# A kernel of a scan and two MoE layers: the range test of the first MoE's weights is moved into the second MoE

## The chip, the cores and the metric

The kernel runs on one core of one Trainium2 chip. A core has five engines that this text names: PE (TensorE, matrix products), DVE (VectorE), ACT (ScalarE), POOL (GpSimd) and SP (SyncE, which issues nearly all transfers). The metric is the device time of one execution in microseconds (us).

## The reference

Inputs are float32 arrays for the scan; the MoE weights arrive as float64, and the kernel converts them itself.

```python
def _attn_ref(r, k, v, w, a, b):          # 4 batches, 8 heads, 768 steps, head size 40
    for t in range(S):
        y[:, :, t] = np.einsum('bhd,bhde->bhe', rt, state)
        Sa = np.einsum('bhde,bhe->bhd', state, at)
        state_decay = state * wt[:, :, None, :] - np.einsum('bhd,bhe->bhde', Sa, bt)
        state = state_decay + np.einsum('bhd,bhe->bhde', vt, kt)

def _moe_ref(x, w1, w2, w3, w_out):       # 3072 tokens, 320 -> 768 -> 320
    h = np.maximum(np.maximum(x @ w1, x @ w2), x @ w3)
    return h @ w_out

def _moe2_ref(x, w_in, w_out):            # 3072 tokens, 320 -> 2048 -> 320
    h = x @ w_in
    sp = np.where(h > 20.0, h, np.log1p(np.exp(np.minimum(h, 20.0))))
    g = h * np.tanh(sp)
    return g @ w_out
```

The output is the scan, then the first MoE, then the second.

## The kernel before

The scan is cut into 48 chunks of 32 steps (24 for each half of the batch). `Attention.pre` (L230 on) prepares pairs of chunks; `Attention.solve` inverts a triangular system of four pairs on DVE (L303 to L314); `Attention.chain` runs one chunk through PE, ACT and DVE. The first solve and the first four `pre` run before the first chunk. In `pre`, PE writes a product `m` into PSUM (L275), ACT copies half of it to `ab` (L280) and DVE transposes the other half to `akT` (L282); `solve` begins with DVE's transpose of `ab` (L303).

The first MoE's weights are 24 tiles: 18 of 128 x 3 x 128 for w1, w2, w3 and 6 of 128 x 320 for w_out. `from64` (L575 on) loads a tile of float64 words into `raw` (SP, L579), tests its range, and turns it into float32 with ACT (L593), DVE (L594, L595) and POOL (L597). The parts `put` then splits it into a high and a low part for the float32 products (ACT L606, POOL L612, DVE L651; for w_out L718 and L721). The test is a pair of ACTIVATEs with an accumulated sum: Square of the high words (L587) and Exp of the result (L588). The sums go to columns of the tile `g_t`, and `Gate.count` compares them with their bounds at the very end: if any bound is broken, a slow general version runs instead. So the test's result is needed only at the end of the kernel.

`pipelined(moe1.weights(), 2)` starts a new tile every second step, and `fill` takes three steps of it in each of the five slots of a chunk, so the conversion lies beside chunks 0 to 3. From chunk 4 on the first MoE runs beside the scan (`Moe1.group`). The second MoE's weights are converted by the same `from64` beside the last chunks and the first MoE's tail, their tests writing into the staging tile (`ct`, `t`).

The second MoE is six groups of 512 tokens (`Moe2.group`). A group has 16 blocks `m`: eight matmuls of 512 columns into `cps` (four PSUM banks, L661 to L665), an elementwise chain that alternates between ACT (L969, L972, L973, L974, L983) and DVE (L970, L976, L977, L979, L984), and twelve matmuls of 320 columns into `cops` (L988 to L990). `cps` of a block is free after DVE's L979. The next group's x is loaded by SP (L933) and split by POOL (L941, L942); the output is copied by DVE (L1024) and ACT (L1026) and stored by SP (L1028).

PE and DVE keep the written order up to the end of the scan. ACT does too, but for chunks 0 to 3, where a conversion's step may be put ahead of a step that is written earlier. Elsewhere a scheduler orders the instructions when the kernel is built, by its own estimate of times. Every engine then runs its list in order, and so does SP's queue.

Of the kernel before, what the change touches and what calls it, by code (L numbers as in the profile page):

```python
# [8 lines left out]
F32 = mybir.dt.float32  # L9
F32R = mybir.dt.float32r  # L10
I32 = mybir.dt.int32
AF = mybir.ActivationFunctionType
ALU = mybir.AluOpType
PSUM = bass.MemoryType.PSUM

B, H, S, D = 4, 8, 768, 40
DM, F1, F2 = H * D, 768, 2048
# [136 lines left out]
class Attention:  # L154
# [74 lines left out]
    def load(self, n):  # L229
        self.load_a(n)  # L230
        self.load_k(n)
# [333 lines left out]
def finish(it):  # L565
    for _ in it:
        pass
# [5 lines left out]
    return stage  # L573


def from64(nc, stage, src, n, cols, gate, put, beside=False, junk=None):

    raw, t = stage(n, cols)
    nc.sync.dma_start(out=raw, in_=src.bitcast(I32).rearrange("p k (f w) -> p k f w", w=2))  # L579
    for _ in range(3 if junk else 2):  # L580
        yield
    low, high = raw[:, :, :, 0], raw[:, :, :, 1]
    tf = t.bitcast(F32)
    q = junk.tile([128, n, cols], F32, name="junk", tag="junk") if junk else tf


    nc.scalar.activation(out=q, in_=high.bitcast(F32), func=AF.Square, accum_out=gate.le(2.0 ** 33))  # L587
    nc.scalar.activation(out=q, in_=q, func=AF.Exp, scale=-(2.0 ** 20), accum_out=gate.le(0.25))  # L588
    yield
    if beside:  # L590
        nc.vector.tensor_scalar(out=low, in0=low.bitcast(mybir.dt.uint32), scalar1=2.0 ** -29, scalar2=None, op0=ALU.mult)
    else:
        nc.scalar.activation(out=low, in_=low.bitcast(mybir.dt.uint32), func=AF.Copy, scale=2.0 ** -29)  # L593
    nc.vector.tensor_scalar(out=t, in0=high, scalar1=3, scalar2=0x3FFFFFF8, op0=ALU.logical_shift_left, op1=ALU.bitwise_and)  # L594
    nc.vector.scalar_tensor_tensor(out=t, in0=high, scalar=-0x40000000, in1=t, op0=ALU.bitwise_and, op1=ALU.bitwise_or)  # L595
    yield
    nc.gpsimd.tensor_tensor(out=t, in0=t, in1=low, op=ALU.add)  # L597
    yield
    yield from put(tf)
# [31 lines left out]
class Weights:  # L631
# [9 lines left out]
        return (x[:, 0:256].rearrange("p (k f) -> p k f", k=2), x[:, 256:512].rearrange("p (k f) -> p k f", k=2),  # L641
                x[:, 512:640])

    def load(self, j, stage, beside=False, pool=False, junk=None):
        nc = self.nc
        h, l, m = self.parts(j)

        def put(t):
            copy(nc, m, t[:, 2], pool)
            yield from split_to(nc, h, l, t[:, 0:2], pool)  # L650
            nc.vector.tensor_tensor(out=m[64:128], in0=t[64:128, 2], in1=m[64:128].bitcast(F32), op=ALU.subtract)  # L651

        return from64(nc, stage, self.src[j], 3, 128, self.gate, put, beside, junk)

    def mm(self, ps, j, x):

# [20 lines left out]
class Moe1:  # L677
    N = 2 * GT

    def __init__(self, ctx, tc, A, xs, x1, gate):  # L680
        self.tc, self.nc, self.A, self.xs, self.x1, self.gate = tc, tc.nc, A, xs, x1, gate

        def pool(name, bufs, ctx=ctx, **kw):
            return ctx.enter_context(tc.tile_pool(name=name, bufs=bufs, side="left", reuse_waits="tile", **kw))

        self.pool = pool
        wp = pool("b_w", 1)
        self.stage = ExitStack()
        self.tmp = staged(pool("b_t", 4, ctx=self.stage))
        self.junk = pool("b_j", 1, ctx=self.stage, space=PSUM)  # L690
        ws = [wp.tile([128, 6, 640], F32R, name="b" + n) for n in ("w1", "w2", "w3")]
        self.w = [Weights(self.nc, A[n], [w[:, j] for j in range(6)], gate) for n, w in zip(("w1", "w2", "w3"), ws)]

        self.o = wp.tile([128, 6, 2, DM], F32R, name="bo").rearrange("p k s f -> p k (s f)")
# [14 lines left out]
    def weights(self):  # L709
        for j in range(6):  # L710
            for w in self.w:
                yield w.load(j, self.tmp, junk=self.junk)
        for j in range(6):
            yield from64(self.nc, self.tmp, self.A["wo"][j], 1, DM, self.gate, lambda t, j=j: self.put_out(t[:, 0], j), junk=self.junk)

    def put_out(self, t, j):
        nc, o = self.nc, self.o[:, j]
# [102 lines left out]
class Moe2:  # L820
# [168 lines left out]
            nc.tensor.matmul(out=self.acc[j], lhsT=gh[:, cs], rhs=self.ol[m], start=False, stop=False)  # L989
            nc.tensor.matmul(out=self.acc[j], lhsT=gl[:, cs], rhs=self.oh[m], start=False, stop=(m == 15))  # L990

    def group(self, q):

        tc, nc = self.tc, self.nc
        acc = self.acc = [self.psb.tile([128, DM], F32, name=f"cops{j}") for j in range(4)]
        rest = iter(()) if q else self.conversions()
        under, self.begun = self.begun, []
        early = len(under)
        for m in range(16 + 3):
            if early <= m < 16 and (q, m) not in self.ps:  # L1000
                self.product(q, m)
            for i, g in enumerate(under):
                if i >= early or m >= i + 1:
                    next(g, None)
            if early <= m < 16:
                under.append(self.activation(q, m))
                next(under[-1])
            if m == 8 and q < 5:
                self.load_x(q + 1)
            if m == 11 and q < 5:  # L1010
                self.split_x(q + 1)

            with tc.issue_after(self.newest):
                next(rest, None)
                if m == 11:
                    finish(rest)
        del self.x[q]
        o = self.p2.tile([128, 4, DM], F32, name="o")
# [158 lines left out]
def program(tc, A, out, only=None):  # L1177
    nc = tc.nc
# [6 lines left out]
    with ExitStack() as c_mid:  # L1185
        keep = c_mid.enter_context(tc.tile_pool(name="keep", bufs=1, side="right"))
        moe2 = Moe2(tc, A, x1, out, gate)
        with ExitStack() as c_moe1:
# [55 lines left out]
                        moe2.begin(i - 18, moe1.spare(i % 2))  # L1244
            finish(rest)
        moe2.open_work(c_mid)
        for q in range(6):
            moe2.group(q)
    if only:
        only(att, xs, x1)  # L1250
    n, total = gate.count()
# [21 lines left out]
```

## Time and profile before

| What | Value |
|---|---|
| median of 3 runs | 1072.19 us |
| lowest and highest | 1071.51 and 1073.66 us |
| span of the profiled execution, first to last instruction | 1070.9 us |
| what lies between the span and the median | 1.3 us |
| PE busy | 912.0 us (85% of the span) |
| DVE busy | 878.3 us (82%) |
| ACT busy | 731.2 us (68%) |
| POOL busy | 339.6 us (32%) |
| moved by DMA | 87.03 MB, 81 GB/s in the mean |

Of the profiled execution the page gives the span; its own time is that span and what lies around it, for which the last difference is taken. The shares are means over stages with different limits, so the stretches below say more than this table. A wait is named after what ended it.

### The profile page before, as it was taken

The page shows a single profiled execution, that of the slowest core. Times are in us where ns is not written, and L with a number is a line of the kernel's source. Part 1 is how long each engine was busy: PE and PEld are TensorE (multiplying, and loading weights), DVE is VectorE, ACT ScalarE, POOL GpSimd, SP SyncE. Part 2 cuts the span into 40 slices and gives each one's busy share as a digit, 9 for nine tenths or more (in the row PEclk, how much of TensorE's full clock was granted, in tenths as well). Part 3 has the DMA queues.
Part 4 walks back from the last instruction along what each step waited for, and adds up shares of the span by engine and source line. Part 5 has one row for each costly group of instructions (what it writes and reads, how often), then busy time and mean ns, then how long its engine had stood idle before and what let it go on. Part 6 is the DMA issues. An engine that isn't in the chain of part 4 may idle for free.

```text
span 1070.9 us, 34069 instructions
## 1 busy us (share of the span) xinstructions
PE 912.0 (85%) x14098; PEld 816.2 (76%) x14098; DVE 878.3 (82%) x1698; ACT 731.2 (68%) x1886; POOL 339.6 (32%) x422
## 2 busy tenths in 40 slices
PE   1313456899999999999999999979999999999996
PEld 1212345888888888888998888878889998888995
DVE  7589979978968987886688666899988989898875
ACT  4638864465566665656667777677787887878874
POOL 7437894333233242323114334681201002010000
PEclk9999999999999999999999999999999999999999
DMA  8415532243433434333334443530100000010000
GB/s 211 134 62 159 144 91 64 71 128 84 114 101 100 110 96 113 94 88 97 81 85 104 132 134 90 173 108 5 30 25 31 25 30 26 1 54 1 25 1 28
DMA packets 110615, 87.03 MB, mean 81 GB/s; under 512 B 72740, under 2 KB 89764, under 8 KB 110452
## 3 DMA queue, kind: packets, MB, share of 16 engines
q1 hardware_dynamic: 109712, 84.54, 29.0%
q8 instruction: 113, 1.85, 0.8%
q14 instruction: 50, 0.41, 0.1%
q10 hardware_dynamic: 740, 0.23, 0.1%
HBM read 72.16 MB, written 12.58 MB: 79 GB/s over the span
## 4 chain that ended last, share of the span: by engine, by line
PE 56%; DVE 23%; ACT 9%; issue 4%; DMA 4%; POOL 2%; SPq 0%; ACTq 0%; DVEq 0%; POOLq 0%
PE cops L988 5%; PE cops L989 5%; PE cops L990 5%; PE ys L436 4%; PE bps L661 4%; PE cps L661 4%; PE cps L662 4%; PE cps L663 4%; PE bps L812 3%; DVE T L310 3%; PE bps L662 3%; PE bps L663 3%; DVE tv L308 3%; PE cgps L353 2%; PE cps L665 2%
## 5 line engine op out<-in xcount | busy, mean ns | idle before, releaser
L661 PE MATMUL bps<-bxh,bw 128*128 128x256 f32 x432 | 139.9, 325 | 2.3 <-DVE mx L771 1.4
L662 PE MATMUL bps<-bxl,bw 128*128 128x256 f32 x432 | 124.1, 287 | 3.2 <-DVE bxl L674 3.2
L663 PE MATMUL bps<-bxh,bw 128*128 128x256 f32 x432 | 122.8, 284 | 0.0
L774 POOL TENSOR_TENSOR hl<-mx,hh 128x256 fp32r<-128x256 f32 x72 | 56.7, 787 | 172.8 <-ACT hh L773 145.2
L310 DVE TENSOR_TENSOR T<-T,tv 128x31 f32<-128x31 f32 (+15 forms) x186 | 86.4, 464 | 6.4
L661 PEld LDWEIGHTS bps<-bxh,bw 128*128 128x128 f32 x432 | 82.5, 191 | 11.4 <-DVE mx L771 2.0
L252 POOL TENSOR_TENSOR ax<-ax,pp 40x256 f32<-40x256 f32 x96 | 75.4, 805 | 45.1 <-DMA ax<-in_A_dram 16.1
L662 PEld LDWEIGHTS bps<-bxl,bw 128*128 128x128 f32 x432 | 83.2, 193 | 5.4 <-DVE bxl L674 5.4
L288 POOL TENSOR_SCALAR_AFFINE_SELECT ax<-akT 32x256 f32<-32x256 f32 x96 | 51.3, 535 | 104.6 <-DVE akT L282 100.6
L663 PEld LDWEIGHTS bps<-bxh,bw 128*128 128x128 f32 x432 | 83.1, 192 | 0.0
L972 ACT ACTIVATE e<-e 128x512 f32<-128x512 f32 x93 | 58.6, 630 | 33.3 <-DVE e L970 33.0
L436 PE MATMUL ys<-rs,ls 128*40 128x72 f32 x1536 | 64.8, 241 | 14.6 <-DVE rs L423 9.9
L812 PE MATMUL bps<-hh,bo 128*128 128x256 f32 x360 | 74.9, 291 | 1.5 <-ACT mx L769 1.5
L984 DVE TENSOR_TENSOR gl<-e,gh 128x512 fp32r<-128x512 f32 x93 | 65.8, 708 | 12.5 <-ACT gh L983 12.5
L976 DVE SCALAR_TENSOR_TENSOR e<-e,r 128x512 f32<-128x512 f32 x93 | 66.0, 710 | 11.7 <-ACT r L974 11.4
L275 PE MATMUL m<-bk,ax 40*32 40x64 f32 x1536 | 43.1, 254 | 38.1 <-DMA bk<-in_KB_dram 14.6
L436 PEld LDWEIGHTS ys<-rs,ls 128*40 128x40 f32 x1536 | 55.6, 126 | 22.0 <-DVE rs L423 9.4
L441 DVE TENSOR_TENSOR sv<-ys,pp 40x320 f32<-40x320 f32 x92 | 44.7, 486 | 32.1 <-PE ys L436 31.4
L941 POOL CAST cxh<-cxl 128x1536 fp32r<-128x1536 f32 x5 | 9.1, 1814 | 193.8 <-DMA cxl<-x 193.8
L771 DVE TENSOR_TENSOR mx<-bps,mx 128x256 f32<-128x256 f32 x144 | 60.3, 419 | 11.6 <-ACT mx L769 7.7
L977 DVE SCALAR_TENSOR_TENSOR e<-e,r 128x512 f32<-128x512 f32 x93 | 68.2, 734 | 1.0
L308 DVE TENSOR_TENSOR tv<-tr,T 128x31 f32<-128x31 f32 (+15 forms) x186 | 67.1, 361 | 1.9
(214 smaller groups left out, 3108.3 us busy)
## 6 DMA issues: line engine op xcount, KB each, us to landing
bk<-in_KB_dram SPq DMA_DIRECT2D x24, 448.0 KB
sv<-in_SV_dram SPq DMA_DIRECT2D x96, 80.0 KB
raw<-in_w_dram SPq DMA_DIRECT2D x18, 384.0 KB
w<-in_W_dram SPq DMA_DIRECT2D x21, 231.0 KB
v<-in_VT_dram SPq DMA_DIRECT2D x48, 96.0 KB
rs<-in_RT_dram SPq DMA_DIRECT2D x48, 96.0 KB
cxl<-x SPq DMA_DIRECT2D x12, 384.0 KB
raw<-in_wo_dram SPq DMA_DIRECT2D x13, 320.0 KB
```

What stands on the lines that cost most here:

```text
L252: nc.gpsimd.tensor_tensor(out=xv[:, h], in0=xv[:, h], in1=P[ro, h, 0:C], op=ALU.mult)
L308: nc.vector.tensor_tensor(out=tv, in0=abT[:, s, s + 1:C].unsqueeze(2).to_broadcast([128, n, s + 1]), in1=T[:, s, 0:s + 1].unsqueeze(1).to_ ...
L310: nc.vector.tensor_tensor(out=T[:, s + 1:C, 0:s + 1], in0=T[:, s + 1:C, 0:s + 1], in1=tv, op=ALU.subtract)
L436: nc.tensor.matmul(out=self.ys[64 * y:64 * y + 40, p, 0:72], lhsT=l[:, y, p], rhs=r_[:, :, 4 * (p % 4) + 2 * (1 - y) + p // 4], start=True ...
L661: nc.tensor.matmul(out=ps, lhsT=h[:, k], rhs=xh[:, k], start=(k == 0), stop=False)
L662: nc.tensor.matmul(out=ps, lhsT=h[:, k], rhs=xl[:, k], start=False, stop=False)
L663: nc.tensor.matmul(out=ps, lhsT=l[:, k], rhs=xh[:, k], start=False, stop=False)
L771: after(1, lambda ps=ps, mx=mx: nc.vector.tensor_tensor(out=mx, in0=ps, in1=mx, op=ALU.max))
L812: nc.tensor.matmul(out=pss[d][rows], lhsT=lhsT, rhs=rhs, start=first, stop=last)
L976: nc.vector.scalar_tensor_tensor(out=e, in0=e, scalar=1.0, in1=r, op0=ALU.add, op1=ALU.mult)
L977: nc.vector.scalar_tensor_tensor(out=e, in0=e, scalar=-float(np.sqrt(8.0)), in1=r, op0=ALU.add, op1=ALU.mult)
L984: nc.vector.tensor_tensor(out=gl, in0=e, in1=gh.bitcast(F32), op=ALU.subtract)
```

## The change

The test becomes a function of its own, `test64`. With `later=True`, `from64` leaves it out, and with it one of its steps; the first MoE's 24 tiles are converted in that way. A new generator, `Moe1.tests`, loads each of the 24 tiles once more into the second MoE's staging tiles and does the same two ACTIVATEs there, with the result in `t`. `Moe2.group` takes a step of it in each of its 19 turns in groups 1 to 5, a new tile every third step. The PSUM tile `junk` goes.

```diff
+def test64(nc, high, q, gate):
+
+    nc.scalar.activation(out=q, in_=high.bitcast(F32), func=AF.Square, accum_out=gate.le(2.0 ** 33))
+    nc.scalar.activation(out=q, in_=q, func=AF.Exp, scale=-(2.0 ** 20), accum_out=gate.le(0.25))
+
+
+def tested(nc, stage, src, n, cols, gate):
 
     raw, t = stage(n, cols)
     nc.sync.dma_start(out=raw, in_=src.bitcast(I32).rearrange("p k (f w) -> p k f w", w=2))
-    for _ in range(3 if junk else 2):
+    for _ in range(3):
+        yield
+    test64(nc, raw[:, :, :, 1], t.bitcast(F32), gate)
+
+
+def from64(nc, stage, src, n, cols, gate, put, beside=False, later=False):
...
+    for _ in range(3 if later else 2):
         yield
     low, high = raw[:, :, :, 0], raw[:, :, :, 1]
     tf = t.bitcast(F32)
-    q = junk.tile([128, n, cols], F32, name="junk", tag="junk") if junk else tf
-
-
-    nc.scalar.activation(out=q, in_=high.bitcast(F32), func=AF.Square, accum_out=gate.le(2.0 ** 33))
-    nc.scalar.activation(out=q, in_=q, func=AF.Exp, scale=-(2.0 ** 20), accum_out=gate.le(0.25))
-    yield
+    if not later:
+        test64(nc, high, tf, gate)
+        yield
...
-        self.junk = pool("b_j", 1, ctx=self.stage, space=PSUM)
...
+    def tests(self, stage):
+
+        for j in range(6):
+            for n in ("w1", "w2", "w3"):
+                yield tested(self.nc, stage, self.A[n][j], 3, 128, self.gate)
+        for j in range(6):
+            yield tested(self.nc, stage, self.A["wo"][j], 1, DM, self.gate)
...
-    def group(self, q):
+    def group(self, q, rest):
...
-        rest = iter(()) if q else self.conversions()
...
                 next(rest, None)
-                if m == 11:
+                if m == 11 and q == 0:
                     finish(rest)
...
+        tests = pipelined(moe1.tests(moe2.stage), 3)
         for q in range(6):
-            moe2.group(q)
+            moe2.group(q, tests if q else moe2.conversions())
+        finish(tests)
```

At three places this is how the lists of instructions change. The lines of the changed kernel are numbered anew: L587 and L588 are L578 and L579 there, L593 is L605, L933 is L952, L969 is L988.

ACT before the first solve, before the change (`m_330` and `m_374` are the products of the third and the fourth `pre`):

```order
L587 ACTIVATE junk,g_t<-raw 128x384
L260 ACTIVATE tr_167,g_t<-tr_167 104x16x32
L593 ACTIVATE raw<-raw 128x384
L246 ACTIVATE Q,g_t<-Q 104x512
L588 ACTIVATE junk,g_t<-junk 128x384
L593 ACTIVATE raw<-raw 128x384
L280 COPY ab_155<-m_330 128x256
```

and the same place with the change, down to the copy of the fourth:

```order
L605 ACTIVATE raw<-raw 128x384
L260 ACTIVATE tr_164,g_t<-tr_164 104x16x32
L246 ACTIVATE Q,g_t<-Q 104x512
L605 ACTIVATE raw<-raw 128x384
L280 COPY ab_152<-m_327 128x256
L605 ACTIVATE raw<-raw 128x384 x2
L280 COPY ab_152<-m_371 128x256
```

The tests ahead of the first copy are gone; between the two copies stood, before, six more instructions of tests besides the two L593, and now only these two.

ACT in the second MoE, behind the first group's output copy, before the change:

```order
L969 ACTIVATE e<-cps 128x512
L972 ACTIVATE e<-e 128x512
L983 CAST gh<-e 128x512
L973 ACTIVATE r<-e 128x512
L969 ACTIVATE e<-cps 128x512
L974 ACTIVATE r<-r,half 128x512
```

and with the first of the 24 tests:

```order
L992 ACTIVATE r<-e 128x512
L988 ACTIVATE e<-cps 128x512
L578 ACTIVATE t_12898,g_t<-raw 128x384
L993 ACTIVATE r<-r,half 128x512
L579 ACTIVATE t_12898,g_t<-t_12898 128x384
L1002 CAST gh<-e 128x512
```

A test's two ACTIVATEs stand between the steps of the elementwise chain, in most places one pair for every three blocks, and now and then two within one block; the last pair stands in the list a little before the fifth group's output copy.

SP's queue from the first group's stores to the second's, before the change:

```order
L1028 DMA out_dram<-o 128x2x320 x2
L933 DMA cxl<-x_0_76 128x3x256
L933 DMA cxl<-x_1_77 128x3x256
L1028 DMA out_dram<-o 128x2x320 x2
L933 DMA cxl<-x_2_78 128x3x256
```

and with the change:

```order
L1046 DMA out_dram<-o 128x2x320 x2
L585 DMA raw<-in_w_dram 128x768 x4
L952 DMA cxl<-x_0_76 128x3x256
L952 DMA cxl<-x_1_77 128x3x256
L585 DMA raw<-in_w_dram 128x768 x3
L1046 DMA out_dram<-o 128x2x320 x2
```

Seven loads of weights stand among a group's loads of x and its stores, and each needs one of three staging buffers, which the test of three tiles earlier frees.

## Rows read from the trace of the kernel before

**Rows 1.** Busy time by stretch: length, busy us (instructions) by engine, granted clock, DMA share, GB/s.
```profile
69.00:170.00 101.00, 43.36 (x1146) 34.93 (x1138) 87.16 (x136) 75.11 (x242) 80.17 (x92) 1.00 0.45 126
170.00:200.00 30.00, 22.80 (x405) 20.07 (x408) 26.93 (x57) 12.13 (x38) 9.72 (x14) 0.89 0.28 70
...
300.00:400.00 100.00, 96.64 (x2222) 87.66 (x2220) 82.03 (x185) 62.63 (x195) 36.63 (x58) 1.00 0.40 101
...
790.00:848.00 58.00, 58.00 (x323) 52.31 (x322) 51.31 (x83) 47.78 (x83) 5.84 (x2) 1.00 0.08 26
```

**Rows 2.** Lines L587 and L588, tests: duration ns min/median/max, first and last start.
```profile
L587 ACT ACTIVATE junk<-raw x24: 438/508/535, 32.0 to 146.8; 128x384 f32<-128x384 f32 x18, 128x320 f32<-128x320 f32 x6
L587 ACT ACTIVATION_READ_ACCUMULATOR junk<-raw x24: 185/188/207, 32.5 to 147.2; 128x1 f32 x24
...
L588 ACT ACTIVATE junk<-junk x24: 415/474/488, 34.2 to 147.7; 128x384 f32<-128x384 f32 x18, 128x320 f32<-128x320 f32 x6
```

**Rows 3.** ACT's groups by shape, whole run: busy us, mean ns | idle before.
```profile
L587 ACT ACTIVATE t<-raw 128x384 f32<-128x384 f32 x6 | 3.3, 553 | 3.1 <-DMA raw<-in_wi_dram 3.1
...
L588 ACT ACTIVATE t<-t 128x384 f32<-128x384 f32 x6 | 3.1, 515 | 0.0
```

**Rows 4.** Instructions in time order, 31 to 41 us: start us, length us [idle before <-releaser].
```profile
31.99 0.54 ACT L587 ACTIVATE junk<-raw 128x384 f32<-128x384 f32 x1
...
34.20 0.47 ACT L588 ACTIVATE junk<-junk 128x384 f32<-128x384 f32 x1
...
35.12 0.35 ACT L280 COPY ab<-m 128x256 f32<-128x256 f32 x1
...
36.08 2.49 PE L275 MATMUL m<-bk,ax 40*32 40x64 f32 x64 [2.99 <-DVE akT L282]
...
39.85 0.36 ACT L280 COPY ab<-m 128x256 f32<-128x256 f32 x1
...
40.30 0.45 DVE L282 STREAM_TRANSPOSE akT<-m 128x256 f32<-128x256 f32 x1 [3.70 <-ACT ab L280]
```

**Rows 5.** Groups by line, 69 to 170 us.
```profile
L587 ACT ACTIVATE junk<-raw 128x384 f32<-128x384 f32 (+1 forms) x20 | 9.9, 497 | 2.8 <-DMA raw<-in_w_dram 2.6
```

**Rows 6.** DVE's waits, 69 to 160 us: us in total, times, longest.
```profile
DVE bw L651 <- ACT bw L606: 4.0, 3, 1.8
DVE sv L441 <- PE ys L436: 2.6, 2, 1.9
...
DVE w L256 <- ACT Q L246: 0.5, 1, 0.5
```

**Rows 7.** ACT in time order, second MoE's first groups.
```profile
778.58 0.73 ACT L1026 COPY o<-cops 128x320 f32<-128x320 f32 x2
...
784.19 0.63 ACT L972 ACTIVATE e<-e 128x512 f32<-128x512 f32 x1
...
787.06 0.63 ACT L972 ACTIVATE e<-e 128x512 f32<-128x512 f32 x1
...
836.23 0.74 ACT L1026 COPY o<-cops 128x320 f32<-128x320 f32 x2
```

**Rows 8.** Time order around two of POOL's splits of x: ACT; POOL, DVE and PE.
```profile
831.50 0.63 ACT L972 ACTIVATE e<-e 128x512 f32<-128x512 f32 x1 [2.43 <-DVE e L970]
...
943.18 3.84 POOL L942 TENSOR_TENSOR cxl<-cxl,cxh 128x1536 fp32r<-128x1536 f32 x1
...
943.67 3.89 DVE L977 SCALAR_TENSOR_TENSOR e<-e,r 128x512 f32<-128x512 f32 x1
947.60 0.69 DVE L979 SCALAR_TENSOR_TENSOR e<-e,cps 128x512 f32<-128x512 f32 x1
...
948.34 0.50 PE L661 MATMUL cps<-cxh,c_ax 128*128 128x512 f32 x1 [0.70 <-DVE e L979]
```

**Rows 9.** SP's issue of the last x, and PE's first matmul on it.
```profile
936.86 1.19 SPq L933 DMA_DIRECT2D cxl<-x  x2
...
995.97 0.40 PE L661 MATMUL cps<-cxh,c_ax 128*128 128x512 f32 x1
```

More of the change, by code (lines that the diff above doesn't have):

```diff
@@ L573, in staged @@
     return stage
-def from64(nc, stage, src, n, cols, gate, put, beside=False, junk=None):
+def test64(nc, high, q, gate):
+    nc.scalar.activation(out=q, in_=high.bitcast(F32), func=AF.Square, accum_out=gate.le(2.0 ** 33))
+    nc.scalar.activation(out=q, in_=q, func=AF.Exp, scale=-(2.0 ** 20), accum_out=gate.le(0.25))
+def tested(nc, stage, src, n, cols, gate):
     raw, t = stage(n, cols)
     nc.sync.dma_start(out=raw, in_=src.bitcast(I32).rearrange("p k (f w) -> p k f w", w=2))
-    for _ in range(3 if junk else 2):
+    for _ in range(3):
+        yield
+    test64(nc, raw[:, :, :, 1], t.bitcast(F32), gate)
+def from64(nc, stage, src, n, cols, gate, put, beside=False, later=False):
+    raw, t = stage(n, cols)
+    nc.sync.dma_start(out=raw, in_=src.bitcast(I32).rearrange("p k (f w) -> p k f w", w=2))
+    for _ in range(3 if later else 2):
         yield
@@ L642, in parts, with load @@
                 x[:, 512:640])
-    def load(self, j, stage, beside=False, pool=False, junk=None):
+    def load(self, j, stage, beside=False, pool=False, later=False):
         nc = self.nc
@@ L651, in put @@
             nc.vector.tensor_tensor(out=m[64:128], in0=t[64:128, 2], in1=m[64:128].bitcast(F32), op=ALU.subtract)
-        return from64(nc, stage, self.src[j], 3, 128, self.gate, put, beside, junk)
+        return from64(nc, stage, self.src[j], 3, 128, self.gate, put, beside, later)
     def mm(self, ps, j, x):
@@ L711, in weights @@
             for w in self.w:
-                yield w.load(j, self.tmp, junk=self.junk)
+                yield w.load(j, self.tmp, later=True)
         for j in range(6):
-            yield from64(self.nc, self.tmp, self.A["wo"][j], 1, DM, self.gate, lambda t, j=j: self.put_out(t[:, 0], j), junk=self.junk)
+            yield from64(self.nc, self.tmp, self.A["wo"][j], 1, DM, self.gate, lambda t, j=j: self.put_out(t[:, 0], j), later=True)
+    def tests(self, stage):
[4 more added lines that the diff above has]
+            yield tested(self.nc, stage, self.A["wo"][j], 1, DM, self.gate)
     def put_out(self, t, j):
```

## The prediction

> **What bounds the kernel now.** I read the busy time by stretch first [rows 1]. The reader is to see two regimes. From 69 to 170 us, while the first MoE's weights are converted beside the first attention chunks, no engine is full: DVE is busy for 87.16 of 101 us, POOL for 80.17, ACT for 75.11 and PE for 43.36. From 300 us on PE is the limit (96.64 of 100), and in the second MoE it is not idle in a whole group (58.00 of 58), with DVE at 51.31 and ACT at 47.78. The change takes ACT work out of the first regime and puts it into the second.
>
> Then the cost of a test. Before, the two ACTIVATEs last 508 and 474 ns in the median, and an accumulator read of 188 ns follows [rows 2]; with the same read behind the second that is 1.36 us, and 24 tiles make 32.6 us of ACT. In the second MoE the result goes to the staging tile t and no longer to the PSUM tile junk; the tests that already write t last 553 and 515 ns for 128x384 [rows 3], so a tile costs 1.44 us there, and 24 make at most 34.7 us.
>
> **The change part by part.**
>
> *1. The start.* The first triangular solve cannot begin before the fourth pre-step is done. Its chain runs through ACT [rows 4]. Before the copy ab at 35.12 stand an L587 of 0.54 and an L588 of 0.47; without them the copy, and the matmuls m behind it at 36.08, come 1.0 us sooner. These matmuls end at 36.08 + 2.49 = 38.57, but the next copy ab starts only at 39.85, for ACT is still at tests: 1.3 us more. DVE's transpose akT at 40.30, which waited 3.70 us, hangs on that copy, and the solve follows it. So the solve starts 1.0 + 1.3 - 0.1 (a hand-over) = 2.2 us sooner. It is pure DVE work until the first chunk, so I carry the whole 2.2 us. Lower end 1.0 (only the first part), upper end 2.4.
>
> *2. The conversion stretch.* 20 of the 24 tests lie here [rows 5], 20 x 1.36 = 27 of ACT's 75.11 us. DVE keeps its written order, so only its waits can shrink. Three of them lead to ACT [rows 6]: 4.0 us for the casts L606 that queue among the tests, 0.5 us for Q, and 2.6 us for matmuls whose inputs ACT copied: 7.1 us. The tests are 27/75 = 36% of what a step queues behind on ACT, which gives 2.6 us. I take 3.3, a little more, because each conversion also loses one step and so frees its buffers sooner. The ends are 0 (DVE and POOL hold the pace) and 7.1. Behind this stretch the work is one chain and then PE-bound, so I count on the shift lasting: 2.2 + 3.3 = 5.5 us.
>
> *3. ACT in the second MoE.* The copies of a group's output are at 778.58 and 836.23 [rows 7]: 57.65 us for 16 blocks, 3.60 us per block. Where ACT is packed, L972 follows L972 after 787.06 - 784.19 = 2.87 us [rows 7], five operations whose durations sum to about 3.2. So ACT is 0.73 us per block faster than PE. A test enters every third block; packed like the others (2.87/3.2) it takes 1.3 us. Three blocks then need 3 x 2.87 + 1.3 = 9.9 us of ACT against 10.8 of PE. PE stays the bound on average, but ACT catches up with 0.3 us per block and no longer 0.73.
>
> This matters once per group. POOL splits the next x: its subtraction L942 runs 3.84 us, and a DVE step that overlaps it takes 3.89 us where the next one takes 0.69 [rows 8]. The lead of the elementwise work over PE then falls to nothing, and in one group PE waits 0.70 us [rows 8]. Two or three tests fall between this split and the lowest lead, 2.6 to 3.9 us of ACT. At another split ACT has a hole of 2.43 us [rows 8], which tests can fill in part. What is left is 0.2 to 1.5 us per transition; I take 0.75, and four transitions carry tests: 3.0 us. Lower end 0; upper end, with no hole filled, 4 x 3.9 = 15.6.
>
> *4. Transfers.* 18 x 384 KB and 6 x 320 KB are read once more, 9.0 MB. The group from 790 to 848 moves 26 GB/s at a DMA share of 0.08, while the stretch from 69 to 170 moves 126 GB/s [rows 1]; 9.0 MB over four groups of 58 us add 39 GB/s. I take nothing. The Trainium skill (SBUF — State Buffer, "A bandwidth-pool intuition that's wrong (but worth ruling out)") says that HBM is almost always the end-to-end bottleneck; by that rule the extra reads would be paid in full. On SP's queue the new loads stand ahead of the loads of x and of the output stores, and one that waits for a staging buffer holds them up. The x of the last group is issued at 936.86 and its first matmul runs at 995.97 [rows 9]: 59 us, of which POOL's split takes under 10, so about 50 us cover it. If that cover went, a group would start late by what exceeds it.
>
> *5. The rest at nothing.* The two counting instructions on the 56 test columns move from the first group to the last on DVE, whose 51.31 us are 7 under PE's 58.00 [rows 1]. The last test stands a group before the end, so the final count waits for nothing new. The granted clock is 0.89 in the mean from 170 to 200 [rows 1], so TensorE spent some 6 us there at the level of 1.2 GHz, after a stretch in which PE was busy 43%; the dip may move or go, which I price at 2 us to either side and keep in the range.
>
> *Sum.* The profiled execution's span is 1070.9 us, and the median of the runs is 1072.19, 1.3 us above it. 1070.9 - 5.5 + 3.0 + 1.3 = **1069.7 us**.
>
> **The rivals.** A measurement of this kernel can tell about 0.2% (2.1 us) from no change.
>
> *The tests are free where they land.* If ACT's holes take them all, term 3 is 0: 1066.7, and down to 1063 with more of the 7.1 us of term 2. For it: PE is at 58.00 of 58, ACT at 47.78 [rows 1]. Against it: the hole at the split is smaller than the tests that fall near it.
>
> *DVE and POOL hold the pace of the conversion.* Then term 2 is 0 and 1072.2 - 2.2 + 3.0 = 1073.0. For it: DVE is the busiest engine of that stretch, and POOL comes before ACT as well [rows 1]. Against it: 4.5 us of DVE's waits name ACT itself [rows 6]. The Trainium skill (Perfetto Trace Analysis, "Identifying the Most-Contended Engine") says to optimise the engine with the highest occupancy first; by that rule taking work off ACT here gives nothing, which is this case. The waits speak against the strict form of it.
>
> *ACT becomes the bound behind each split (slower).* The place is the eight or so blocks after POOL's subtraction, where ACT now gains only 0.3 us per block. If the 2.43 us hole is not filled, because the tests stand behind the blocked operation in ACT's order, two tests per transition reach PE: 4 x 2.6 = 10.4, so 1072.2 - 5.5 + 10.4 = 1077. It decides once the lead does not return to about 4 us before the next split: 16 blocks x 0.3 = 4.8 us is just enough. For it: PE already waits there [rows 8]. Against it: the average still leaves 0.9 us per three blocks.
>
> *The transfers bind.* If the 9.0 MB did not overlap, at 126 GB/s they would cost 72 us: 1144. The share of 0.08 [rows 1] speaks against it. This is the case of the SBUF page of the Trainium skill.
>
> That the change does not do what it says can be left out: the instruction order shows the tests gone from the start and present in the second MoE's groups.
>
> **How the numbers follow.** The forecast has 0.42, the free tests 0.15, the held pace 0.22, ACT as the bound 0.19, the transfers 0.02. The forecast's own range, 1067 to 1071.5, is mostly under 1070.05 (0.30) and partly within 0.2% (0.12). The free tests are all faster. The held pace is within 0.2% for 0.16 and slower for 0.06. The last two are slower. That is 0.45 faster, 0.28 same, 0.27 slower. The range reaches from the upper half of the free tests, 1064.5, to just over ACT as the bound, 1077.5; below and above lie less than 2 in 10.
>
> **What would show each step.** The transpose akT ahead of the first solve should stand near 38.1 us (was 40.30), and the end of the conversion near 5 us sooner; DVE's wait for L606 should fall from 4.0 us to about 2. PE should still be at 58 of 58 within a group, with waits for DVE's last step of 0.5 to 1.5 us behind each split. The forecast is wrong if the first solve does not move, if a gain at 170 us is gone at 700, or if PE loses more than 2 us per group.

## The result and the profile after

| | kernel before | changed kernel |
|---|---|---|
| median of 5 runs | 1072.19 us | 1078.14 us |
| span of the profiled execution | 1070.9 us | 1076.2 us |
| ratio, with its 95% interval | | 1.0072 (1.0050 to 1.0094) |

The changed kernel is slower by 0.72%, 7.7 us; 1069.7 us and a gain had been forecast. 0.1% is 1.07 us in what follows. The ratio is taken over all executions; the two medians differ by 6.0 us and the two profiled executions by 5.2, and a comparison of the two profiles can account only for the last.

Three things can be read from the profile after. First the busy time by stretch, with the columns of [rows 1]:

```profile
69.00:170.00 101.00, 41.86 (x1112) 34.12 (x1104) 86.92 (x134) 52.67 (x155) 76.95 (x90) 1.00 0.43 130
170.00:200.00 30.00, 23.54 (x460) 20.83 (x458) 26.87 (x59) 13.06 (x41) 9.70 (x14) 0.89 0.23 57
...
670.00:735.00 65.00, 54.05 (x335) 48.74 (x334) 62.99 (x103) 44.92 (x121) 41.97 (x42) 0.95 0.35 111
...
790.00:848.00 58.00, 57.25 (x314) 50.94 (x313) 51.07 (x82) 51.47 (x109) 5.36 (x2) 1.00 0.21 68
```

In the conversion ACT (the fourth busy time) fell from 75.11 to 52.67 us. POOL fell by 3.2 us, and DVE, the busiest, stands at 86.92, where it was at 87.16 [rows 1]. In a group of the second MoE PE is idle for 0.75 us of 58 where it was idle for none, and ACT carries 3.7 us more. From 670 to 735 us the mean granted clock is 0.95: this is the passage from the first MoE into group 0, where no late test runs.

Then the start, in time order, against [rows 4]; the last line is from the kernel before:

```profile
30.43 0.27 ACT L389 COPY X<-x0ps 128x160 f32<-128x160 f32 x1
...
32.72 0.35 ACT L280 COPY ab<-m 128x256 f32<-128x256 f32 x1
...
36.22 0.37 ACT L280 COPY ab<-m 128x256 f32<-128x256 f32 x1 [1.14 <-PE m L275]
36.68 0.45 DVE L282 STREAM_TRANSPOSE akT<-m 128x256 f32<-128x256 f32 x1 [2.48 <-ACT ab L280]
```

```profile
31.68 0.27 ACT L389 COPY X<-x0ps 128x160 f32<-128x160 f32 x1
```

The second copy now waits for its matmuls and no longer for ACT's queue, and the transpose ahead of the solve stands at 36.68 in place of 40.30. Of these 3.6 us, 1.2 are an earlier launch of everything (the first chunk's copy X, L389, is at 30.43, was 31.68), which has nothing to do with the tests: the kernel before with another order at the passage (part 3) has this copy at 30.40. From that copy to the transpose it is 6.25 us, was 8.62, so 2.4 us are the tests'.

Last the waits of PE in the groups, 735 to 1060 us, with total, times and longest; first the kernel after, then the kernel before:

```profile
PE cps L673 <- DVE e L998: 2.0, 4, 0.6
PE cops L1009 <- DVE gl L1003: 1.4, 2, 1.1
PE cops L1007 <- ACT o L1044: 0.5, 1, 0.5
```

```profile
PE cps L661 <- DVE e L979: 0.7, 1, 0.7
```

3.9 us against 0.7 belong to the price of the late tests, but these rows are no full measure of it: without any late test they still sum to 1.6 us (first run of part 1). The instructions that both kernels share give a better one. From ACT's output copy of group 0 to that of the last group it is 288.0 us after and 283.7 before: 4.3 us.

They also tell where the rest went. Against the kernel before, the chunks of the scan stand 1.9 us earlier at 265 us and 4.2 earlier at 608; the output copies of group 0 (at 778.58 before [rows 7]) stand 0.8 us later. In stretches: 1.2 us from the earlier launch; the scan, from the first copy X to the last, takes 625.8 us in place of 628.9; the passage, from that copy to group 0's output copy, takes 123.1 in place of 118.0. With the 4.3 us of the groups that is the difference of 5.2 us between the two profiles. So the gain of the scan, and more, is lost at the passage. (Of the scan's 3.0 us, 1.4 come between 561 and 575 us, where the kernel before had a lower clock, as shown below.) It reads so there, on POOL, DVE, DVE and PE:

```profile
715.99 3.87 POOL L961 TENSOR_TENSOR cxl<-cxl,cxh 128x1536 fp32r<-128x1536 f32 x1
...
716.49 3.91 DVE L996 SCALAR_TENSOR_TENSOR ce<-ce,spare 128x512 f32<-128x512 f32 x1
...
720.43 0.43 DVE L822 TENSOR_TENSOR mx<-bps,mx 64x256 f32<-64x256 f32 x1
...
720.91 0.64 PE L1007 MATMUL cops<-c_ax,gh 128*128 128x320 f32 x1 [4.98 <-DVE mx L822]
```

L822 is DVE's evacuation of the first MoE's last piece; it frees the PSUM bank that the fourth cops needs. In DVE's order it stands behind L996 (L977 of the kernel before), a step of 0.7 us that POOL's subtraction for group 1's x holds for 3.91. PE waits 4.98 us. In the kernel before the same instructions stand in the same order on POOL and on DVE, and pass each other:

```profile
717.88 1.88 POOL L941 CAST cxh<-cxl 128x1536 fp32r<-128x1536 f32 x1 [0.93 <-DMA cxl<-x]
...
721.23 3.48 POOL L942 TENSOR_TENSOR cxl<-cxl,cxh 128x1536 fp32r<-128x1536 f32 x1
...
717.42 0.41 DVE L970 TENSOR_SCALAR e<-e 128x512 f32<-128x512 f32 x1
...
720.23 0.77 DVE L977 SCALAR_TENSOR_TENSOR ce<-ce,spare 128x512 f32<-128x512 f32 x1
721.04 0.43 DVE L803 TENSOR_TENSOR mx<-bps,mx 64x256 f32<-64x256 f32 x1
721.50 0.69 DVE L979 SCALAR_TENSOR_TENSOR ce<-ce,cps 128x512 f32<-128x512 f32 x1
722.10 2.90 DVE L970 TENSOR_SCALAR e<-e 128x512 f32<-128x512 f32 x1
...
721.52 0.41 PE L988 MATMUL cops<-c_ax,gh 128*128 128x320 f32 x1 [1.55 <-DVE mx L803]
```

There x landed late: POOL's cast waited 0.93 us for the transfer, and the subtraction began 1.0 us after L977, the step that it holds in the changed kernel, where it began 0.5 us before it. L977 was through in 0.77 us, and the evacuation had started 0.2 us before the subtraction. What the subtraction then held, L970, stands behind the evacuation. I call the first case the meeting.

The granted clock differs as well. These are 10 us pieces, first of the kernel after, then of the kernel before:

```profile
710.00:720.00 10.00, 5.19 (x25) 3.90 (x23) 10.00 (x10) 7.17 (x17) 7.96 (x5) 0.97 0.33 109
720.00:730.00 10.00, 9.09 (x39) 8.50 (x40) 9.84 (x17) 6.14 (x11) 3.41 (x4) 0.69 0.19 54
```

```profile
560.00:570.00 10.00, 8.09 (x175) 7.28 (x174) 9.52 (x24) 6.09 (x21) 4.39 (x5) 0.89 0.51 132
570.00:580.00 10.00, 10.00 (x203) 9.15 (x204) 8.00 (x21) 7.00 (x24) 3.80 (x5) 0.94 0.28 68
```

Around the end of PE's wait of 5 us, to about 726.4 us, TensorE was granted 1.2 GHz: the mean of 0.69 leaves 3.1 us of the second ten lost. The kernel before had a shorter stretch of that kind near 568 us, which the kernel after has not.

### The profile page after: what moved, and what is told of

Same layout as the page of the kernel before. It is cut to its first block, busy times and chain, and to the rows that moved or that the text cites. A ratio compares the mean times of both kernels' runs of the same rounds, so it can differ in the third digit from the quotient of the medians.

```text
span 1076.2 us, 34123 instructions
## 1 busy us (share of the span) xinstructions
PE 913.6 (85%) x14098; PEld 816.7 (76%) x14098; DVE 885.6 (82%) x1698; ACT 725.4 (67%) x1886; POOL 337.2 (31%) x422
## 5 line engine op out<-in xcount | busy, mean ns | idle before, releaser
L675 PE MATMUL bps<-bxh,bw 128*128 128x256 f32 x432 | 122.3, 283 | 0.0
L288 POOL TENSOR_SCALAR_AFFINE_SELECT ax<-akT 32x256 f32<-32x256 f32 x96 | 50.8, 529 | 104.0 <-DVE akT L282 100.0
L995 DVE SCALAR_TENSOR_TENSOR e<-e,r 128x512 f32<-128x512 f32 x93 | 71.0, 763 | 13.1 <-ACT r L993 13.1
L1003 DVE TENSOR_TENSOR gl<-e,gh 128x512 fp32r<-128x512 f32 x93 | 71.0, 764 | 9.8 <-ACT gh L1002 8.6
L1002 ACT CAST gh<-e 128x512 fp32r<-128x512 f32 x93 | 57.0, 613 | 20.8 <-DVE e L998 20.7
L389 ACT COPY X<-x0ps 128x160 f32<-128x160 f32 x48 | 14.0, 292 | 79.9 <-PE x0ps L386 79.7
```

Of the source, the lines that this page charges most:

```text
L675: nc.tensor.matmul(out=ps, lhsT=l[:, k], rhs=xh[:, k], start=False, stop=False)
L995: nc.vector.scalar_tensor_tensor(out=e, in0=e, scalar=1.0, in1=r, op0=ALU.add, op1=ALU.mult)
L1002: nc.scalar.copy(out=gh, in_=e)
L1003: nc.vector.tensor_tensor(out=gl, in0=e, in1=gh.bitcast(F32), op=ALU.subtract)
```

## The experiments

The theory that went into the first runs: (A) the late tests cost PE some 4.7 us behind the splits, and (B) the meeting costs some 5 us at the passage. Each run's ratio is against runs of the kernel before on the same chip, five rounds, with its 95% interval. A difference of two ratios carries both intervals, 0.2 to 0.3% as a rule. A trace is of one execution: in nine kernels whose early part is that of the changed kernel, the scan takes 625.6 to 628.6 us.

**1. Which part of the change does it.** In the changed kernel, first no late tests and loads, then the loads alone:

```diff
-        tests = pipelined(moe1.tests(moe2.stage), 3)
+        tests = iter(())
```
```diff
     for _ in range(3):
         yield
-    test64(nc, raw[:, :, :, 1], t.bitcast(F32), gate)
```

> The changed kernel without the late tests and their loads: the 24 tiles of the first MoE's weights are not tested at all. Theory: two separate losses. (A) The late tests on ACT cost PE about 4.7 us behind the four splits of groups 1 to 4. (B) About 5 us go at the passage into group 0, where no late test runs: the scan ends about 4 us earlier, and POOL's subtraction for group 1's x then runs beside a DVE step that stands ahead of DVE's evacuation of the first MoE's last piece. If so, this run keeps the scan's gain of about 4 us and the loss at the passage, loses only the 4.7 us, and takes about 1073.4 us, ratio about 1.001 against the kernel before; its trace still shows PE waiting about 5 us near 716 us. Rival: the late tests cause both losses; then the time is about 1068 us, ratio 0.996, and no such wait is there.

> The changed kernel with the late loads of the 24 tiles, but without their two ACTIVATEs: those tiles are not tested. Order of PE, DVE, ACT and POOL is that of the run without late tests; only SP's queue and the 9 MB differ. Theory: transfers cost nothing, so within 1 us of the run without late tests (about 1073.4 us). Rival: the transfers or SP's queue are what delays groups 1 to 5; then it is within 1 us of the changed kernel (1078 us).

Measured: 1.0043 (1.0021 to 1.0065) and 1.0037 (1.0016 to 1.0058). Without any late test the kernel is still slower than before, and PE's wait is still there:

```profile
723.99 0.63 PE L1007 MATMUL cops<-c_ax,gh 128*128 128x320 f32 x1 [4.55 <-DVE mx L822]
```

So the passage is not the tests' doing (rival out), and the 9 MB of loads cost nothing that shows. The late tests are 1.0072 - 1.0043 = 0.29%, 3.1 us, which the two intervals alone don't tell from zero; the traces do better, with 283.3 us in both runs from group 0's output copy to the last group's, against 288.0 in the changed kernel: 4.7 us. The first ratio was 0.33%, 3.5 us, over what was expected: I had read a gain of 4 us in the scan from one profile. In the trace of this run the scan takes 628.6 us, as in the kernel before (628.9).

**2. The late part alone**, on the kernel before (`tested`, `tests` and the `rest` argument as in the change, early tests kept, a wider `g_t`):

```diff
+        tests = pipelined(moe1.tests(moe2.stage), 3)
         for q in range(6):
-            moe2.group(q)
+            moe2.group(q, tests if q else moe2.conversions())
+        finish(tests)
```

> The kernel before with the late loads and tests added, the early tests kept: the scan is as before. Theory: the scan ends as before, so POOL's subtraction does not meet the evacuation, and only the late tests' 4.7 us show: about 1077 us, ratio 1.0044. If the late tests also caused the loss at the passage: about 1082 us, ratio 1.009. If they cost nothing at all: 1072 us.

Measured: 1.0060 (1.0034 to 1.0086), 1077.57 us, between the two expectations. I had expected no meeting, for the scan is as before. The trace has one:

```profile
717.50 1.79 POOL L964 CAST cxh<-cxl 128x1536 fp32r<-128x1536 f32 x1
...
717.89 1.69 DVE L993 TENSOR_SCALAR e<-e 128x512 f32<-128x512 f32 x1
...
720.50 3.86 POOL L965 TENSOR_TENSOR cxl<-cxl,cxh 128x1536 fp32r<-128x1536 f32 x1
...
720.99 3.91 DVE L1000 SCALAR_TENSOR_TENSOR ce<-ce,spare 128x512 f32<-128x512 f32 x1
...
725.42 0.63 PE L1011 MATMUL cops<-c_ax,gh 128*128 128x320 f32 x1 [4.79 <-DVE mx L826]
```

POOL's cast waits for no transfer here and starts 0.4 us earlier than in the kernel before, while DVE is 0.5 us later: its L993 (L970 of the kernel before) now starts behind the cast, not ahead of it. The first wording of (B), that the scan's earlier end brings the meeting about, falls: a shift of 0.9 us between POOL and DVE is enough, about as much as the kernel before's cast had waited for x.

**3. The meeting, taken apart.** First POOL's subtraction in three pieces, in the changed kernel:

```diff
-            self.nc.gpsimd.tensor_tensor(out=lo, in0=lo.bitcast(F32), in1=hi.bitcast(F32), op=ALU.subtract)
+            for k in range(3):
+                self.nc.gpsimd.tensor_tensor(out=lo[:, k], in0=lo[:, k].bitcast(F32), in1=hi[:, k].bitcast(F32), op=ALU.subtract)
```

> The changed kernel with POOL's subtraction of each split cut into three of 512 columns; nothing else moves on PE, DVE or ACT. Theory: DVE's step is held for about 1.3 us instead of 3.9, the evacuation comes 2 to 2.6 us sooner, PE's wait falls from 5 us to about 2.5, the granted clock does not fall behind it (3.4 us), and the waits behind the later splits shrink by half (about 2 us): about 1070 to 1072 us, ratio 0.998 to 1.000. Rival: POOL's pieces follow one another so closely that DVE gets no turn, or the wait comes from elsewhere: 1078 us as the changed kernel.

Measured: 1.0039 (1.0018 to 1.0060). DVE's step fell from 3.91 to 1.75 us and PE's wait from 4.98 to 2.82, as expected; the clock fell all the same (0.83 from 720 to 730 us), and the time won less than expected (0.998 to 1.000).

Then the evacuation put ahead of the step that is held, by an edge from L996 of the last early block to it; in the changed kernel, in the kernel before, and in the changed kernel without late tests:

```diff
+                self.last = nc.vector.tensor_tensor(out=o[0:M], in0=pss[d][64:128], in1=o[0:M], op=ALU.add).ins
...
+        with behind(first):
             nc.vector.scalar_tensor_tensor(out=e, in0=e, scalar=-float(np.sqrt(8.0)), in1=r, op0=ALU.add, op1=ALU.mult)
...
-                    if 18 <= i < 18 + NE:
+                    if 18 <= i < 17 + NE:
                         moe2.begin(i - 18, moe1.spare(i % 2))
+            moe2.begin(NE - 1, moe1.spare((17 + NE) % 2), moe1.last)
```

> The changed kernel with DVE's evacuation of the first MoE's last piece put ahead of the one DVE step that POOL's subtraction holds for 3.9 us; until there every engine's order is that of the changed kernel. Theory (the loss at the passage is the meeting of the two): the evacuation ends near 716.5 us in place of 720.9, PE's wait of 5 us there falls under 1 us and the granted clock does not fall behind it; DVE is still held, so 1 to 3 us of the 8 may come back as waits in group 0. Ratio 1.000 to 1.003 against the kernel before, where the changed kernel has 1.007. Rival (the wait has another cause, or DVE's delay only moves on to group 0): 1.006 or more.

> The kernel before with the same evacuation put first. Theory: in its profile the subtraction began 0.2 us after the evacuation, because group 1's x landed 0.9 us late, so there is little to win: ratio 0.998 to 1.001. Rival: most executions of the kernel before meet as the changed one does, and the profiled one was the exception: ratio 0.995 or less, and then the passage explains nothing of the difference between the kernels.

> The changed kernel without the late tests (the 24 tiles are not tested) and with the evacuation first. It holds the gain of the early part alone. Theory: the scan's gain of 2 to 4 us stands, with nothing lost at the passage or in the groups: ratio 0.996 to 0.999. Rival (the early gain is not real, or is lost again wherever the scan ends): 1.000 or more.

Measured: 1.0032 (1.0018 to 1.0047), 1.0005 (0.9991 to 1.0019) and 0.9988 (0.9970 to 1.0007). In the changed kernel with this order:

```profile
717.61 3.92 POOL L961 TENSOR_TENSOR cxl<-cxl,cxh 128x1536 fp32r<-128x1536 f32 x1
...
718.21 0.43 DVE L822 TENSOR_TENSOR mx<-bps,mx 64x256 f32<-64x256 f32 x1
718.56 3.52 DVE L997 SCALAR_TENSOR_TENSOR ce<-ce,spare 128x512 f32<-128x512 f32 x1
...
718.70 0.41 PE L1008 MATMUL cops<-c_ax,gh 128*128 128x320 f32 x1 [1.14 <-DVE mx L822]
```

The subtraction has begun, and the evacuation goes through beside it in 0.43 us: one of its two inputs is in PSUM. The step behind it is held for 3.52 us. PE's wait is 1.14 us in place of 4.98, and 1.0072 - 1.0032 = 0.40%, 4.3 us, come back; without late tests it is 1.0043 - 0.9988 = 0.55%, 5.9 us. The passage agrees: it takes 122.3 to 123.9 us in the four kernels so far with a meeting and the subtraction whole, 117.7 and 116.2 in these two changed ones with the evacuation first. The clock, though, falls in the first of them too (0.83 from 720 to 730 us), which had not been expected. The same order gives the kernel before nothing, from which I conclude that it mostly escaped the meeting. (B) is shown as the order's doing, at 4 to 6 us. With the passage mended, the late tests are 1.0032 - 0.9988 = 0.44%, 4.7 us (2.5 us by the traces, 286.9 against 284.4 us from group 0's output copy to the last group's), and the gain of the scan is 1.0005 - 0.9988 = 0.17%, 1.8 us, no more than its uncertainty.

The Trainium skill (SBUF — State Buffer, "SBUF: two separate sides") says that DVE and GpSimd share one pair of ports under an exclusive lock, which binds, among others, a DVE operation with two SBUF inputs and is held for the whole instruction. The rows agree: 3.91 and 3.52 us beside 3.87 and 3.92 of POOL, and 0.43 for the step that reads PSUM. A step with a single input in SBUF was held as well: L970 of the kernel before, 2.90 us beside POOL's 3.48, 0.41 at 717.42.

**4. The late tests: the split, or the place.** The subtraction in three pieces and the evacuation first, in the changed kernel and in the kernel before:

> The changed kernel with the evacuation first and POOL's subtraction of each split in three pieces. Theory: DVE's steps are held 1.3 us at a time, so the waits of PE behind the later splits (about 5 us in the changed kernel) fall by half: 2 us below the run with the evacuation first alone, ratio 0.998 to 1.001. Rival: those waits are ACT's queue, not DVE's hold, and the pieces change nothing: the same ratio as that run within 0.001.

> The kernel before with the evacuation first and POOL's subtraction in three pieces: the same two aids that the changed kernel had in the last run, so that the move of the tests is compared on equal ground. Theory: the kernel before has little to win from them (its PE waits 1.2 us behind the splits and 5 us in group 0): ratio 0.997 to 0.9995, so the move of the tests is worth within 0.2% of nothing once both losses are mended. Rival: the aids help both kernels alike, 0.4% or more: ratio 0.996 or less, and the move stays a loss.

Measured: 0.9996 (0.9980 to 1.0013) and 0.9980 (0.9961 to 0.9999). The pieces win 0.36% in the changed kernel and 0.25% in the kernel before, each give or take some 0.2%. So both are helped, and on equal ground, 0.9996 against 0.9980, the move of the tests is worth nothing that can be told from zero, and no gain.

Then the tests kept away from the splits, with the subtraction whole and in three pieces:

```diff
-                next(rest, None)
+                if q in (0, 5) or not 10 <= m <= 16:
+                    next(rest, None)
...
-        tests = pipelined(moe1.tests(moe2.stage), 3)
+        tests = pipelined(moe1.tests(moe2.stage), 2)
```

> The changed kernel with the evacuation first and POOL's splits whole, but no step of the late tests in the turns 10 to 16 of groups 1 to 4, and a new tile every second turn in place of every third. The same 24 tests on ACT, away from the splits. Theory A (a test hurts where it stands between a split and PE's lowest lead): most of the 4.7 us comes back, ratio 0.9995 to 1.001. Rival (ACT's work in a group counts, wherever it stands, for it sets the lead that the split eats): 1.003, as with the evacuation first alone.

> The last kernel with the subtraction in three pieces as well. If the late tests can be had at no cost at all, this is the version: ratio 0.998 to 0.999, the gain of the scan and nothing lost. If it is 0.9996 or more, the place of the tests adds nothing to the pieces.

Measured: 1.0004 (0.9987 to 1.0021) and 1.0003 (0.9987 to 1.0020). The waits of PE from 735 to 1060 us in the first of the two, in one row:

```profile
PE cops L1008 <- ACT gh L1003: 1.9, 1, 1.9
```

All 24 tests run on ACT, and no wait is left behind any split; the one row is the last block's. From group 0's output copy to the last group's it is 284.2 us, against 286.9 with the tests at their old place and 284.4 without late tests. (A) holds: 0.28% of the 0.44% come back by the place alone. The pieces add nothing to that. Whether the remaining 0.16% against the run without late tests is real, the intervals don't tell. The move stays no gain: on the chip of these runs the median is 1069.42 us for the kernel before with both aids and 1072.32 us for the changed kernel with both and the tests away from the splits.

**5. The early part: the start of the solve, or the conversion.** The kernel before with the evacuation first and only the first four tiles untested, whose tests stand ahead of the solve; and the opposite, the changed kernel with the evacuation first, no late tests, and these four tested at their old place:

```diff
-                yield w.load(j, self.tmp, junk=self.junk)
+                yield w.load(j, self.tmp, junk=self.junk, test=3 * j + k >= 4)
```
```diff
-                yield w.load(j, self.tmp, later=True)
+                yield w.load(j, self.tmp, later=True, junk=self.junk if 3 * j + k < 4 else None)
```

> The kernel before with the evacuation first, and only the first four tiles untested: the ones whose tests stand ahead of the first solve on ACT. The other 20 are tested in the conversion as before, none late. Theory: the whole gain of the scan comes from the solve, none from the conversion, which DVE and POOL pace: the first chunks stand about 3 us earlier near 139 us in the trace, as with all 24 tests gone, and the ratio is 0.998 to 1.000. Rival (each gives its share, as predicted): under 2 us earlier at 139 us.

> The changed kernel with the evacuation first and no late tests, but with the first four tiles tested at their old place, ahead of the first solve. So 20 tiles are not tested: those whose tests lie in the conversion. Theory: the conversion's tests cost nothing where they were, DVE and POOL pace that stretch; the transpose ahead of the solve goes back to near 40 us, the chunk near 139 us stands within 1 us of the kernel before, and the ratio is that of the kernel before with the evacuation first, 0.999 to 1.0015. Rival (term 2 of the prediction, 3.3 us): the chunk near 139 us stands 2 to 3 us earlier and the ratio is 0.997 to 0.998.

Measured: 0.9977 (0.9960 to 0.9994) and 0.9987 (0.9970 to 1.0004). Counted from the first copy X, which takes the launch out, the second chunk's copy comes after 51.72 us in the kernel before, 49.49 with four tiles untested, 50.27 with all 24 untested (the third run of part 3), and 51.97 with the other 20 untested. So by the traces the whole gain is the start's, and taking the tests out of the conversion gives 0.8 us of it back. Single executions vary here (51.3 to 52.5 us in four kernels with all early tests, 50.3 to 50.8 in nine with none), but the end of the scan says the same: from the first copy X to the last it takes 626.8 to 632.2 us with all early tests, 629.2 with 20 tiles untested, 625.6 to 628.6 with none tested, and 624.1 where only the first four are untested, as in part 6. The ratios don't tell 20 untested (0.9987) from 24 (0.9988). DVE's waits from 69 to 160 us show the same, in the changed kernel, against [rows 6]:

```profile
DVE sv L441 <- PE ys L436: 4.1, 2, 3.2
DVE bw L663 <- ACT bw L618: 4.0, 2, 2.7
...
DVE w L256 <- ACT Q L246: 0.8, 1, 0.8
```

The wait for ACT's casts is 4.0 us as before with 22 us less on ACT, and the wait for ys grew from 2.6 to 4.1. Of the 4.0 us, 1.24 hang, in both kernels, on a cast that waits for POOL's sum. The other 2.74, where it was 1.84 and 0.94, read so on ACT and DVE:

```profile
89.71 0.63 ACT L244 ACTIVATE Q<-pp 104x512 f32<-104x512 f32 x1 [2.27 <-DVE bk L265]
...
92.34 0.59 ACT L618 CAST bw<-t 128x128 fp32r<-128x128 f32 x2
...
92.66 0.29 DVE L663 TENSOR_TENSOR bw<-t,bw 64x128 fp32r<-64x128 f32 x1 [2.74 <-ACT bw L618]
```

and in the kernel before

```profile
91.11 0.65 DVE L594 TENSOR_SCALAR t<-raw 128x384 int32<-128x384 int32 x1
...
91.79 1.25 DVE L595 SCALAR_TENSOR_TENSOR t<-raw,t 128x384 int32<-128x384 int32 x1
...
94.88 0.29 DVE L651 TENSOR_TENSOR bw<-t,bw 64x128 fp32r<-64x128 f32 x1 [1.84 <-ACT bw L606]
```

The cast stands in ACT's order behind Q, which waits for DVE's own L265. Without a test between them ACT is faster, 2.9 us from L265's end to the cast's end in place of 3.9. But in the kernel before DVE filled that time with two steps of the conversion, 1.9 us; now none stands there. What ACT did with its time is in its own waits of the same stretch:

```profile
ACT bw L618 <- POOL t L609: 7.8, 9, 2.0
ACT raw L605 <- DMA raw<-in_w_dram: 7.2, 5, 3.2
...
ACT raw L605 <- DMA raw<-in_wo_dram: 5.1, 5, 1.6
```

The casts wait 7.8 us for POOL's sums, where in the kernel before it was

```profile
ACT bw L606 <- POOL t L597: 4.1, 8, 0.9
```

and the two rows for the loads of raw sum to 12.3 us, where ACT's waits for them summed to 3.5. The ten kernels without tests in the conversion have DVE's two waits within 0.3 us of these, and 6.5 to 8.8 us of the casts' wait for POOL; with four tiles untested the wait for ys is 2.6 as before. The ratio of the run with 20 untested is 0.9987 where 0.9990 to 1.0015 was expected. Its chunk at 230 us stands where it stood before, its last chunk 0.7 us earlier and its last outputs 2.3; most of that lies behind the scan and is within what the interval leaves open.

**6. The gain without the loss.** The kernel before with both aids of part 4, and the first four tests behind ACT's last copy ab ahead of the first solve; every tile is tested, nothing is read twice:

```diff
-        nc.scalar.copy(out=self.ab[:, i:i + 8], in_=psv[:, :, C:2 * C])
+        self.copied = nc.scalar.copy(out=self.ab[:, i:i + 8], in_=psv[:, :, C:2 * C]).ins
...
+        self.gate.start = self.copied
...
+    with gate.tc.issue_after(gate.start):
         nc.scalar.activation(out=q, in_=high.bitcast(F32), func=AF.Square, accum_out=gate.le(2.0 ** 33))
```

> The kernel before with the evacuation first, the subtraction in three pieces, and the tests of the first four tiles put behind ACT's last copy ahead of the first solve. Nothing is left out and nothing is read twice; PE, DVE and POOL keep the order of the run of the kernel before with both aids (0.998). Theory: all that the change could win is the start of the solve, and ACT has room behind it: the transpose stands near 37 us, ratio 0.995 to 0.997, faster than both kernels. Rival: the gain of the start is lost again in the conversion, for the first four staging tiles are held longer: 0.998 as without it.

Measured: 1065.55 us, ratio 0.9945 (0.9926 to 0.9965): faster than both kernels, and by a little more than expected. On ACT the tests now fill the time of the solve:

```profile
36.58 0.37 ACT L280 COPY ab<-m 128x256 f32<-128x256 f32 x1 [0.65 <-PE m L275]
...
40.11 0.51 ACT L589 ACTIVATE junk<-raw 128x384 f32<-128x384 f32 x1
```

## Why the prediction was wrong, point by point

*1. The start: 2.2 us.* Right in mechanism and size: 2.4 us from the copy X to the transpose. It lasts, too: 0.9945 against 0.9980 is 0.35%, 3.7 us, and 0.9977 against 1.0005 is 3.0, each give or take 2 to 3 us; that is if anything more than I gave.

*2. The conversion stretch: 3.3 us.* This step failed; the traces show no gain there. I took 36% of the waits that lead to ACT, because the tests are 36% of ACT's work. But a wait that ends with ACT is not a wait for ACT's queue: 1.24 us of the casts' 4.0 hang on POOL's sum, and in the other 2.74 ACT itself had waited for DVE. The rival that DVE and POOL hold the pace had it right, and even it was too kind, for the new order of the steps lengthens the wait for ys by 1.5 us. The Trainium skill (Perfetto Trace Analysis, "Identifying the Most-Contended Engine") says to optimise the engine with the highest occupancy first. The runs agree with it here, where DVE is the busiest, and at the start too, where ACT is busy for 9.67 of the 10 us from 31 to 41 in the kernel before and DVE for 3.23.

*3. ACT in the second MoE: 3.0 us.* Mechanism right, size about right or a little low: 3.1 and 4.7 us by the two pairs of runs, 4.7 and 2.5 by their traces. The place, between a split and the lowest lead, is shown by the run with the tests away from it.

*4. Transfers: 0.* Right: 1.0037 with the loads and 1.0043 without. The Trainium skill (SBUF — State Buffer, "A bandwidth-pool intuition that's wrong (but worth ruling out)") has HBM almost always as the end-to-end bottleneck, which the prediction read as the reads being paid for; here no run shows a cost.

*5. "Behind this stretch the work is one chain and then PE-bound, so I count on the shift lasting."* This is the step that failed by the most. At the passage the work is not one chain: POOL's split runs on x's arrival and DVE's evacuation on its own order, and in the kernel before's profile the step that can be held began 1.0 us ahead of the subtraction. The meeting cost 4.3 to 5.9 us and was in no term. It did not turn the sign alone: with the evacuation first the changed kernel is still 1.0032, for the scan gave 1.8 us where 5.5 were forecast, and the late tests cost 4.7 where 3.0 were. I had the prices at hand, a held step of 3.89 us [rows 8], but looked for them only where the tests were to stand.

The sum by the runs: -1.8 for the scan, where -5.5 was forecast, +4.7 for the late tests, where it was +3.0, and +4.3 for the passage, where it was nothing: 7.2 us over the kernel before with the evacuation first. The three are steps from one measured ratio to the next, so they add up by themselves; the traces, one execution of each kernel, have -4.3 (of which 1.2 is the launch), +4.3 and +5.1. Slower had a chance of 0.27, nearly all of it from ACT as the bound and the held pace; neither holds the passage. The time came out 0.6 us above the range's upper end of 1077.5.

What stays open is the clock's share. The five profiles with a wait of 2.8 us or more at the passage all have a granted clock under 1 between 700 and 730 us; of the eleven with a shorter one five have it as well. So the drop is not the meeting's alone, and I don't count its 3 us apart from the 4.3.

## What to carry to other kernels

Before counting on a shift to last, look along the program for pairs of instructions that pass each other by less than the shift, above all a long POOL operation and a DVE step with the evacuation behind it; put what PE waits for ahead of what can be held. A share of an engine's work is no share of a wait that names it: ask what the last instruction before the wait's end was itself waiting for. When a change bundles a gain at one place with a cost at another, try the smallest move that keeps the gain; here, with the same two aids in both kernels, four tests moved by a few microseconds did what 24 tests and 9 MB moved by 700 us did not.

## What the runs showed of the hardware

The landing of one transfer varies enough to choose between two orders of events. From the issue of group 1's x to POOL's cast it is 5.8 us in the kernel before, which waited for the transfer, and 5.0 us in the kernel with the tests twice, which did not; the second has the meeting, and its passage is 4.3 us longer. In the nine kernels with the changed early part the cast follows the issue by 5.36 to 5.37 us and never waits for the transfer, so there POOL's own order decides.

A lower granted clock comes for some microseconds at places that change between nearly equal kernels: near 185 us and near 565 us in most profiles, between 700 and 730 us in ten of sixteen. In the rows of the two kernels one costs 1.7 us (560 to 580 us before: 0.89 and 0.94 of two tens) to 3.4 us (710 to 730 us after: 0.97 and 0.69), as much as the terms in question. PE had stood idle since 715.9 us ahead of the second, and was busy for 0.32 of the 2 us from 564 to 566 ahead of the first. So the clock's row is read before two profiles are compared.
